# Loading and turning the first batch of q and k: 1 KB pieces, products into every fourth column, and a gate ahead of GpSimd's loads

## The chip, the cores and the metric

The kernel runs on one core of a Trainium2 chip. What counts is the device time of one execution in microseconds (us). The core's engines each work through a queue of their own: TensorE (PE) does matrix products, VectorE (DVE) and ScalarE (ACT) do elementwise work and empty PSUM, GpSimd (POOL) does some set-up and issues most loads, SyncE (SP) issues the other transfers. Sixteen DMA engines move the data.

## The reference

Attention over a sliding window with a distance bias, followed by a token mixer:

```python
B, H, S, D = 8, 8, 576, 64
scores = (q @ k^T) / 8                       # per batch and head
rel = i - j;  mask = (0 <= rel < 128)
scores = where(mask, scores - slope[h] * |rel|, -1e9)
x = softmax(scores) @ v                      # then (B, S, H*D) = (8, 576, 512)
W = ((x @ w_q) @ (x @ w_k)^T) / 8            # d_hyper 64
out = relu(W @ x) @ w_out                    # float32
```

q, k and v are float32, 256 bytes for each token of a head.

## The kernel before, in words

The 576 tokens of a batch are cut into four blocks of 128 and a tail of 64; the tails of two batches share tiles. The work of a batch is a set of small operations, each with a name of kind, batch and part:

- L: a load. Lq, Lk, Lv bring a block of q, k or v, Lt the tails of q and k. GpSimd issues them, with a change of type to fp16 on the way (`nat` for q and k, `vt` for v). Only batch 0's blocks of q and k are loaded by SyncE as fp32 into `natf` (`lf`, line 549) and cast to `nat` by VectorE or ScalarE (Cq, Ck, lines 365 and 367).
- TQ: 16 TensorE transposes per block turn `nat` so that head_dim lies on partitions (`add_tq`, line 361); ETQ empties PSUM into `qkT` (lines 371, 373). TT and ETT do so for the tails. From batch 1 on, one TQ takes two blocks.
- QK (g, u): scores of block g for half u of the heads; EXP on ScalarE (line 674, 128x1024); MUL by the bias tile on VectorE (line 681). `bias` is made on ScalarE from a mask that GpSimd builds, and `biasl` on VectorE from `bias`.
- PV: probabilities times v; X (lines 723, 724) normalises into `x`.
- XT, EXT turn `x`; WQ, EWQ, WK, EWK, G, EG are the mixer's small products; MX and RM give the relu (lines 835, 837); OUT times `w_out`, EO empties it into `osb` (lines 365, 367), DO writes it out (lines 913, 916).

The order on every engine is fixed when the kernel is built: a list scheduler (`Order.solve`) takes the operations with estimated costs, and where several could go next, the one with the lowest number in the table `WANT`. Each engine then runs its queue in that order and waits by semaphores. PSUM is four pairs of banks that the scheduler also assigns. `keep_busy` puts filler products (`fill`, 128x512) ahead of a TensorE operation for which the plan has a gap, in the first 30 us of the plan; the number comes from the gap divided by an assumed duration, 0.43 before `COLD` and 0.216 after it. The fillers write the bank of the operation that follows them, so they wait for that bank to be empty.

The outputs of batches in `LATE` are held in the pool `late` (18 slots, `HELD`, shared with the eight `natf` tiles) and written by GpSimd after all its loads (`d.deps += issues`); the others are written by SyncE. GpSimd's loads also wait for the eighth load before them to land. `pads` (GpSimd memsets of `xtl` and `xT`) must be done before its loads of q, k, v.

Of the kernel before, what the change touches and what calls it, by code (L numbers as in the profile page):

```python
# [14 lines left out]
P = 128  # L15
S = 576
D = 64
H = 8
# [19 lines left out]
HELD = 18  # L38
LATE = (2, 3, 4, 5)
COLD = 8.0  # L40
# [4 lines left out]
    "ident": -516.89, "idh": -64.27, "iota": -947.82, "dist": -823.27, "zeros": -897.48,  # L45
# [251 lines left out]
def kernel(  # L297
# [302 lines left out]
    def add_tq(b, ns, want):  # L600
# [21 lines left out]
        for n in ns:  # L622
            evt[b, n] = ev
# [380 lines left out]
```

## Time and profile before

| | |
|---|---|
| runs | 146.66 us median of 3 (146.28 to 148.61) |
| the profiled execution | 147.05 us, its span 145.3 us |
| busy: PE, DVE, ACT, POOL | 126.8, 116.7, 114.3, 104.8 us |
| DMA packets | 117447, of them 113072 under 512 bytes |
| loads of `natf`, 256 KB each | 8, issued by SP from 0.74 to 8.26 us, 3.0 to 8.0 us to landing |
| loads by GpSimd | first of `natt` at 5.73 us, last issue done at about 105.4 us |
| first EXP | 10.74 us |
| last product | ends about 141.5 us |

In the lines of the profile a time in us is followed by a duration, the engine, the line of the kernel (L674), the operation, the tile written and the tile read, and a count; in brackets stands how long the engine was idle before it, and what ended that. PEclk is the clock granted to TensorE in tenths. The windows give for a stretch the busy time of each engine with the number of instructions. The chain of waits is followed back from the last instruction.

### The profile page before, as it was taken

How to read it: one execution, taken by the hardware profiler on the slowest of the kernel's cores; microseconds unless marked ns; L12 is line 12 of the kernel's file. 1: busy time of each engine (PE TensorE's matmuls, PEld its weight loads, DVE VectorE, ACT ScalarE, POOL GpSimd, SP SyncE). 2: the span in 40 equal slices, each digit the busy share in tenths (PEclk: the TensorE clock that was granted, in tenths of full speed). 3: DMA queues.
4: the chain of work that ended last, by engine and by line, in shares of the span. 5: the costliest groups of instructions: out<-in, count | busy, mean ns of one | idle time of the engine just before them, and what ended most of it. 6: DMA issues, size and time to landing. Idle time of an engine off the chain costs nothing.

```text
span 145.3 us, 5428 instructions
## 1 busy us (share of the span) xinstructions
PE 126.8 (87%) x2315; PEld 80.0 (55%) x2315; DVE 116.7 (80%) x256; ACT 114.3 (79%) x169; POOL 104.8 (72%) x139
## 2 busy tenths in 40 slices
PE   6858858888997899779998997989999999999990
PEld 2224546645774458645674575647767657566340
DVE  6977997599839698959979999799999999991410
ACT  3727895599588976899599986999889989956751
POOL 5999678999986997578999999998977701230000
PEclk9986999999999999999999999999999999999999
DMA  4999999999999999999999999999999941155255
GB/s 103 262 182 180 159 154 144 149 173 154 190 251 186 157 183 218 247 179 155 156 155 156 157 154 157 154 154 151 146 213 399 363 171 72 77 144 207 83 162 202
DMA packets 117447, 25.64 MB, mean 177 GB/s; under 512 B 113072, under 2 KB 114096, under 8 KB 117424
## 3 DMA queue, kind: packets, MB, share of 16 engines
q0 software_dynamic: 106336, 18.49, 155.3%
q1 hardware_dynamic: 11088, 6.82, 16.6%
q8 instruction: 18, 0.29, 0.8%
q14 instruction: 5, 0.04, 0.1%
HBM read 29.62 MB, written 9.44 MB: 269 GB/s over the span
## 4 chain that ended last, share of the span: by engine, by line
PE 48%; DVE 16%; ACT 16%; POOL 7%; DMA 6%; issue 4%; POOLq 0%; DVEq 0%; ACTq 0%
PE pair L358 41%; ACT pt L674 10%; PE pair L361 7%; DMA vt<-in_v_dram 6%; DVE pt L681 3%; DVE x L724 3%; POOL nat L501 2%; DVE rm L837 2%; ACT qkT L371 2%; DVE xT L373 2%; DVE qkT L373 1%; POOL vt L516 1%; DVE inv L723 1%; POOL natt L508 1%; DVE xtl L724 1%
## 5 line engine op out<-in xcount | busy, mean ns | idle before, releaser
L674 ACT ACTIVATE pt<-pair 128x1024 f16<-128x1024 f32 x64 | 62.8, 1038 | 6.1 <-PE pair L358 5.8
L681 DVE TENSOR_TENSOR pt<-pt,bias 128x1024 f16<-128x1024 f16 x48 | 31.7, 683 | 3.3 <-ACT pt L674 3.1
L516 POOL DMA_DIRECT2D vt<-in_v_dram x32 | 29.7, 949 | 3.7 <-DMA nat<-in_k_dram 1.9
L358 PE MATMUL pair<-wout_sb,rm 128*128 128x512 f16 (+1 forms) x132 | 31.5, 373 | 0.7 <-ACT pt L674 0.5
L501 POOL DMA_DIRECT2D nat<-in_q_dram x28 | 25.9, 931 | 3.3 <-DMA vt<-in_v_dram 1.1
L501 POOL DMA_DIRECT2D nat<-in_k_dram x28 | 25.7, 925 | 1.6 <-DMA vt<-in_v_dram 0.5
L358 PE MATMUL pair<-qkT 64*128 64x256 f16 (+2 forms) x320 | 22.8, 254 | 4.0 <-ACT qkT L371 2.6
L358 PE MATMUL pair<-vt,pt 128*128 128x65 f16 x512 | 22.6, 193 | 1.4 <-DMA vt<-in_v_dram 1.0
L358 PEld LDWEIGHTS <-pt 128*128 128x128 f16 x576 | 20.0, 97 | 5.8 <-issue 2.5
L724 DVE TENSOR_TENSOR x<-pair,inv 128x512 f16<-128x512 f32 x32 | 22.1, 691 | 1.1
L365 ACT COPY osb<-pair 128x512 f32<-128x512 f32 (+1 forms) x25 | 14.8, 590 | 6.9 <-PE pair L358 6.7
L371 ACT COPY qkT<-pair 128x1024 f32<-128x1024 f32 (+2 forms) x19 | 16.0, 842 | 4.5 <-PE pair L361 3.5
L358 PEld LDWEIGHTS <-qkT 64*128 64x128 f16 x320 | 11.2, 95 | 12.4 <-issue 5.9
L358 PEld LDWEIGHTS <-rm 128*128 128x128 f16 x132 | 11.4, 97 | 12.0 <-issue 1.1
L913 POOL DMA_DIRECT2D out_dram<-osb x16 | 8.8, 558 | 11.0 <-DVE osb L367 5.4
L361 PEld LDWEIGHTS <-nat 64*128 64x128 f16 x512 | 9.4, 96 | 6.8 <-issue 4.6
L361 PE MATMUL pair<-identh,nat 64*128 64x64 f16 x512 | 11.2, 192 | 1.8 <-DVE x L724 0.4
L358 PE MATMUL pair<-fill 128*128 128x512 f16 x23 | 9.0, 531 | 3.1 <-DVE qkT L373 1.2
L358 PE MATMUL pair<-xT,wqq_sb 128*128 128x256 f16 (+1 forms) x64 | 10.3, 287 | 0.8 <-DVE xT L373 0.8
L681 DVE TENSOR_TENSOR pt<-pt,biasl 128x1024 f16<-128x1024 f16 x16 | 10.8, 683 | 0.2 <-ACT pt L674 0.2
L837 DVE TENSOR_SCALAR rm<-pair 128x512 f16<-128x512 f32 x16 | 10.5, 681 | 0.1
L367 DVE COPY osb<-pair 128x512 f32<-128x512 f32 (+1 forms) x12 | 8.0, 665 | 2.8 <-PE pair L358 2.7
(65 smaller groups left out, 162.7 us busy)
## 6 DMA issues: line engine op xcount, KB each, us to landing
vt<-in_v_dram POOLq DMA_DIRECT2D x32, 128.0 KB, 6.6
out_dram<-osb POOLq DMA_DIRECT2D x16, 256.0 KB, 4.6
out_dram<-osb SPq DMA_DIRECT2D x15, 256.0 KB, 5.4
nat<-in_k_dram POOLq DMA_DIRECT2D x28, 128.0 KB, 6.4
nat<-in_q_dram POOLq DMA_DIRECT2D x28, 128.0 KB, 6.4
natf<-in_q_dram SPq DMA_DIRECT2D x4, 256.0 KB, 4.5
natf<-in_k_dram SPq DMA_DIRECT2D x4, 256.0 KB, 4.8
out_dram<-osb SPq DMA_DIRECT2D x6, 128.0 KB, 2.4
```

Of the source, the lines that this page charges most:

```text
L358: hold(nc.tensor.matmul(*a, **k))
L361: hold(nc.tensor.transpose(*a))
L365: hold(nc.scalar.copy(out_ap, in_ap))
L367: hold(nc.vector.tensor_copy(out=out_ap, in_=in_ap))
L371: hold(nc.scalar.copy(out_ap.bitcast(FP32), in_ap.bitcast(FP32)))
L501: return lambda: nc.gpsimd.dma_start(out=nat_s[b % NNAT][j][n], in_=src[b, :, P * n:P * n + P, :].transpose([1, 0, 2]))
L516: return lambda: nc.gpsimd.dma_start(out=vt_s[b % NV][t][:, :, 0:D], in_=v[b, :, P * t:P * t + P, :].transpose([1, 0, 2]))
L674: nc.scalar.activation(out=pt[:, 0:1024], in_=two(s.bank).rearrange("p e c -> p (e c)"), func=AF.Exp, scale=SCALE)
L681: ENG2[o.eng].tensor_tensor(out=pt[:, 0:1024], in0=pt[:, 0:1024], in1=bt, op=ALU.mult)
L724: nc.vector.tensor_tensor(out=x[r].rearrange("p (g h d) -> p g h d", g=2, h=4), in0=pxv[r, :, :, 0:64], in1=inv[r].unsqueeze(3).broadcast_ ...
L837: hold(nc.vector.tensor_scalar(out=out_ap, in0=in_ap, scalar1=0.0, scalar2=WSCALE, op0=ALU.max, op1=ALU.mult))
L913: q.dma_start(out=out[b, P * st:P * st + P, c], in_=osb)
```

## The change

Batch 0's blocks of q and k come in by another layout. A 256 KB block of q or k is read so that a partition holds four consecutive tokens of a pair of heads: two transfers of 128 partitions (one for each head of the pair), each partition one piece of 1 KB. The cast puts the two heads of a token side by side. TQ then no longer transposes: for each of the four token positions a product of `nat` with the identity writes 64 columns to every fourth fp32 column of PSUM, so that the tokens come out in order, one PSUM bank for each half of the head pairs. Each bank is emptied by an instruction of its own (ETQ0.n.0 and ETQ0.n.1), and a QK of half u waits for its half alone.

SyncE's loads are issued in order of blocks, and a new GpSimd copy of one column of the third load's tile (`seen`) stands ahead of all of GpSimd's loads. Batch 1 joins the batches whose outputs GpSimd writes late; the pool has 23 slots, and every full-width output tile comes from it. `COLD` and a term of `keep_busy` change: 56 fillers instead of 23. The table `WANT` is new throughout, and with it the order on all engines. In the built order these matter for the start:

- GpSimd: `pads` first, then iota, identity and mask, then the copy into `seen`, then the loads; `wq_sb`, which was the first load, is the 15th; vt02, which was the tenth, is the 16th; all eight blocks of batch 1's q and k are within the first twelve.
- ScalarE: the load of the activation table stands behind a wait for the second transfer of the first block, then Cq0.0, then the bias.
- VectorE: Ck0.0, biasl1, ETQ0.0.0, Cq0.1, biasl0, Ck0.1, ETQ0.1.0, Cq0.2, Ck0.2.
- TensorE: 11 fillers, TQ0.0, 5 fillers, TQ0.1, 5 fillers, QK0.0 (two), 4 fillers, TQ0.2, 4 fillers, PV0.0, QK0.1.1, TT0, QK0.1.0, 9 fillers, TQ0.3, PV0.1.
- SyncE: from the fifth block on, each transfer waits until the transfer eight before it has landed.

```diff
-HELD = 18
-LATE = (2, 3, 4, 5)
-COLD = 8.0
+HELD = 23
+LATE = (1, 2, 3, 4, 5)
+COLD = 6.0
+GATE = (0, 1)
...
     def keep_busy(op, last):
         gap = op.start - max(last, op.bank_free, 0.6) - 0.15
-        n = int((gap + 0.3) / (0.43 if op.start < COLD else 0.216)) if gap > 0.1 else 0
+        n = int((gap + 0.5) / (0.43 if op.start < COLD else 0.216)) if gap > 0.1 else 0
...
     def load(name, want, emit, occ, serve, deps):
-        issue = add(*name, want, {"POOL": (occ, occ + 1.5)}, deps, lambda o: emit())
+        issue = add(*name, want, {"POOL": (occ, occ + 1.5)}, [*deps, *gate], lambda o: emit())
...
         def lf(j, n):
             natf = spool.tile([P, DM], FP32, name="natf", tag="late", bufs=HELD)
-            src = (q, k)[j][0, :, P * n:P * n + P, :].transpose([1, 0, 2])
+            src = (q, k)[j][0, :, P * n:P * n + P, :].rearrange("(c e) (g r) d -> e c g (r d)", e=2, r=4)

             def em(o):
-                nc.sync.dma_start(out=natf.rearrange("p (h d) -> p h d", h=H), in_=src)
+                for e in range(2):
+                    nc.sync.dma_start(out=natf[:, 256 * e:256 * e + 256], in_=src[e])

             def cv(o):
-                cp(o.eng, nat_s[0][j][n].rearrange("p h d -> p (h d)"), natf)
-
-            d = add("L" + "qk"[j], 0, f"f{n}", next(i), {"SP": (0.92, 1.55)}, [], em)
-            d = od.add("Q", 0, n, 0.0, {"Q": (0.92, 1.7)}, [d], lambda o: None)
+                cp(o.eng, nat_s[0][j][n].rearrange("p (r e) d -> p e r d", e=2),
+                   natf.rearrange("p (e r d) -> p e r d", e=2, r=4))
+
+            d = add("L" + "qk"[j], 0, f"f{n}", next(i), {"SP": (0.68, 1.3)}, first[-1:], em)
+            first.append(d)
+            d = od.add("Q", 0, n, 0.0, {"Q": (0.66, 1.2)}, [d], lambda o: None)
+            if (j, n) == GATE:
+                gate.append(add("gate", "", "", -50, {"POOL": (0.1, 0.12)}, [d],
+                                lambda o: nc.gpsimd.tensor_copy(out=seen, in_=natf[:, 0:1])))
...
+    def add_tq0(n, want):
+        def quad(o, h):
+            return one((o.bank[0], h)).rearrange("p (j c t) -> p j c t", j=2, c=2)
+
+        def em(o):
+            for j in range(2):
+                for i in range(4):
+                    for h in range(2):
+                        r = slice(64 * h, 64 * h + 64)
+                        mm(quad(o, h)[:, j].rearrange("p c (g i) -> p i c g", i=4)[:, i],
+                           nat_s[0][j][n][r, 2 * i:2 * i + 2, :].rearrange("p a b -> p (a b)"), identh[r, r],
+                           start=True, stop=True)
+
+        t = add("TQ", 0, n, want, pe(0.47), [loads[0, 0, n], loads[0, 1, n], idh], em, banks=2, mode=1)
+        tq[0, n] = t
+        evt[0, n] = []
+        for h in range(2):
+            def ev(o, h=h):
+                cp(o.eng, qkT_s[0][:, :, 2 * h:2 * h + 2, P * n:P * n + P], quad(t, h))
+
+            evt[0, n].append(add("ETQ", 0, f"{n}.{h}", want + 0.6, EV(0.60, 0.69), [t], ev, frees=[t], half=h))
...
-        need = [evt[b, g], evt[b, g + 1]] if g < 3 else [evt[b, 3], ett[b]]
+        need = [evt[b, g][u], evt[b, g + 1][u] if g < 3 else ett[b]]
...
-            held = b in LATE
-            box["o"] = spool.tile([P, n], FP32, name=f"osb{n}", tag="late" if held else f"osb{n}",
-                                  bufs=HELD if held else 5 if n == DM else 2)
+            box["o"] = spool.tile([P, n], FP32, name=f"osb{n}", tag="late" if n == DM else f"osb{n}",
+                                  bufs=HELD if n == DM else 2)
...
-        for ns in ([0], [1], [2], [3]) if b == 0 else ([0, 1], [2, 3]):
+        for n in range(4) if b == 0 else ():
+            add_tq0(n, base(b, 0) - 4 + 1.5 * n)
+        for ns in ([0, 1], [2, 3]) if b else ():
             add_tq(b, ns, base(b, 0) - 4 + 1.5 * ns[0])
```

More of the change, by code (lines that the diff above doesn't have):

```diff
@@ L37 @@
 LAG = 0.5
-HELD = 18
-LATE = (2, 3, 4, 5)
-COLD = 8.0
+HELD = 23
+LATE = (1, 2, 3, 4, 5)
+COLD = 6.0
+GATE = (0, 1)
 WANT = {
-    "ident": -516.89, "idh": -64.27, "iota": -947.82, "dist": -823.27, "zeros": -897.48,
[153 rows of a table removed]
+    "ident": -331.55, "idh": -57.5, "iota": -566.58, "dist": -425.66, "zeros": -434.25, "zerop":
[152 rows of a table added]
 }
@@ L313 @@
     ppool = ctx.enter_context(tc.tile_pool(name="psum", bufs=1, space=bass.MemoryType.PSUM))
+    seen = cpool.tile([P, 1], FP32, name="seen")
     fill = cpool.tile([P, 512], F16, name="fill")
@@ L530 @@
     wts = wto = None
-    late, issues = [], []
+    late, issues, gate, first = [], [], [], []
     loads = {}
@@ L622, in add_tq @@
         for n in ns:
-            evt[b, n] = ev
+            evt[b, n] = [ev, ev]
     def add_tt(pr, want):
```

305 rows, old and new, of the table WANT are left out of this document.

## The prediction

> **What bounds the kernel now.** I read the page, then the chain of waits, the timeline of the first 40 us, the busy time by windows and the DMA issues.
>
> ```profile
> PE 126.8 (87%) x2315; PEld 80.0 (55%) x2315; DVE 116.7 (80%) x256; ACT 114.3 (79%) x169; POOL 104.8 (72%) x139
> PEclk9986999999999999999999999999999999999999
> ...
> PE 48%; DVE 16%; ACT 16%; POOL 7%; DMA 6%; issue 4%; POOLq 0%; DVEq 0%; ACTq 0%
> ```
> ```profile
> 0.00:37.00 37.00, 28.84 (x439) 16.41 (x440) 30.20 (x87) 26.03 (x39) 32.28 (x49) 0.95 1.84 166
> 37.00:141.50 104.50, 97.94 (x1878) 63.63 (x1875) 86.48 (x170) 87.66 (x130) 72.56 (x91) 1.00 1.73 179
> ```
> The second fence (PE, PEld, DVE, ACT, POOL, clock, DMA share, GB/s) splits the run. From 37 us to the last product at 141.5, TensorE is idle 104.50 - 97.94 = 6.6 us: it sets the pace. In the first 37 us it is busy 28.8, 9.0 of it fillers (the page's group of 23), so some 19.8 us is work: about 17 us go in the start, where the change lies.
>
> ```profile
> 12.99 8.91 DMA vt<-in_v_dram
> ```
> ```profile
> 4.38 2.56 ACT L468 ACTIVATE bias<-wm 128x256 f16<-128x256 f32 x8 [2.36 <-POOL wm L426]
> 4.55 1.31 DVE L430 CAST identh<-ident 128x128 f16<-128x128 f32 x1
> 9.45 0.59 ACT L371 COPY qkT<-pair 128x512 f32<-128x512 f32 x1 [2.00 <-PE pair L361]
> 10.74 1.94 ACT L674 ACTIVATE pt<-pair 128x1024 f16<-128x1024 f32 x2 [0.71 <-PE pair L358]
> ...
> 21.94 0.64 PE L358 MATMUL pair<-vt,pt 128*128 128x65 f16 x16 [0.74 <-DMA vt<-in_v_dram]
> 23.86 1.96 ACT L674 ACTIVATE pt<-pair 128x1024 f16<-128x1024 f32 x2 [1.74 <-PE pair L358]
> 28.46 0.64 PE L361 MATMUL pair<-identh,nat 64*128 64x64 f16 x32
> 30.65 5.60 ACT L674 ACTIVATE pt<-pair 128x1024 f16<-128x1024 f32 x6
> ```
> Two limits follow each other. Up to the first EXP at 10.74, it is the row load, cast, turn, evacuation. Then it is GpSimd's load stream: the chain's DMA piece ends in PV0.2 at 21.94, and TQ1.2 at 28.46 has the stream's 17th load under it; six of batch 1's eight EXPs come only after it, and end at 36.25.
>
> **The change, part by part.** *Loads.* Each of eight 256 KB loads becomes two of 128 pieces of 1 KB.
>
> ```profile
> q1 hardware_dynamic: 8320, 2.10, 40.6%
> ```
> ```profile
> q1 hardware_dynamic: 11088, 6.82, 16.6%
> ```
> ```profile
> L913 SPq DMA_DIRECT2D out_dram<-osb x17: 332/332/530, 35.8 to 142.2; - x17
> ```
> The first row is of 0 to 25 us: 40.6% of 25 us is 10.15 us of 16 engines for eight loads in 256-byte pieces, 1.27 us each. Over the run (second row) 24.1 - 10.15 = 13.97 us go to 4.72 MB, or 18 pieces of 256 KB in 2 KB rows, 0.78 us each. 1 KB lies between: I take 0.85, 8 x 0.42 = 3.4 us of DMA time saved (bounds 0 and 3.9). Issues on SP: 16 x 0.33 and gaps, 5.8 us, against the last issue's end at 8.26 before. From the fifth load on, SP also waits for a semaphore lane, that is for loads 1 to 4 to land; with 1 MB under way that costs nothing while it feeds the engines. Landing: 3.0 us for the first load now, 2.0 at least for an output; I take 2.4, so both halves of the first are there at 3.5 (3.1 to 4.1), the last load at about 9.5 (8.5 to 12) against 15.2 now.
>
> *Gate.* The copy into `seen` waits for the third load's first half, about 4.7. GpSimd's own work ahead of it (pads 1.5, iota 0.36, ident 0.5, mask 0.8, no weight load of 0.68) ends about 4.2. Behind it queue all its loads, so its first leaves at 4.8 against 5.73. With SP's 3.4 us less in their way and that 0.9 us, the 17th load lands about 24.5 instead of 28, and the order changes: both rounds of batch 1's q and k are now within the first 12 (about 19 to 20), the wait before TQ1.2 goes; vt02 becomes the 16th (23 to 25), and PV0.2 now stands behind QK1.1. wq_sb, first of all before, comes 15th; its reader wqq has moved too. Each us that the third load is late is one for the whole stream.
>
> *ScalarE.* In the built order the table load, which ran at 0.73 under nothing, stands behind the wait for the first load's second half, ahead of Cq0.0. Its row says 1.28 us: 3.5 + 1.3 + 0.6 gives Cq0.0 done at 5.4, the bias (2.56) at 8.0 instead of 6.94, the first half evacuation at 8.6. TQ0.0 itself hides it: the eleven fillers ahead end at 6.06. By the Trainium skill (ScalarE: Activation LUTs, What ACT_TABLE_LOAD costs) a switch of table also drains for about 1.38 us; the row shows 1.28 and ScalarE then waits, so no run here shows the drain. By it the estimate would be some 1.4 us later here, and the sum 148.5.
>
> *Turning.* TQ0 keeps 16 products of 64 columns per block: 4 x 0.4 us. Writing every fourth fp32 column is in no row; between nothing and twice the time (1.6 us in all), I take nothing, since columns, not bytes, set the rows (0.19 us for fp32 and fp16 outputs alike). Evacuations double: four more of 128x512 fp32, two on ScalarE (0.60 each) and two on VectorE (0.69), 2.6 us, all in the walk below. The permuted cast I take at 0.5 (rows 0.41 to 1.46).
>
> *Pads moved first* end the 1.31 us cast of identh (a like cast takes 0.41 at least), which ran under those memsets: Ck0.0 can end at 4.95. *33 more fillers*, put by a warm pitch of 0.213 us, fall in gaps but stand before real work.
>
> *Walk.* VectorE: biasl1 waits for bias1 (6.7), to 7.45; ETQ0.0.0 8.15; Cq0.1 8.65; biasl0 9.2; Ck0.1 9.75. TensorE: five fillers after the evacuation at 8.6, TQ0.1 to 10.2, five fillers to 11.25 over the two halves of ETQ0.1 (10.95), QK0.0.1 to 11.7: first EXP 11.75, 1.0 later than now. TQ0.2 stands behind four fillers that need EXP0.0.1's bank (12.8), TQ0.3 behind nine and behind Ck0.3 (about 18.2): batch 0's EXPs end about 24.5 against 20.86. But no load is late then: eight EXPs, ETQ1.2 and EWQ0.0 are 9.6 us, so batch 1's end at 34.1 against 36.25. VectorE, from 19.4, has 16.6 us (X, EXT, MULs, ETQ1.0, EWK0) and 1.4 of waits: MUL1 done at 37.4 against 36.97. EWK0 lies at 35.4 in that row, so MX0 starts about 37.2 (29.0 now), OUT0 at 40.5 (33.55 now).
>
> TensorE's account at 40: before, beyond MX0, QK1 and PV1.0, it has done four OUT (4.1), PV1.1 to 1.3 (1.9), XT1.0 (0.4): 6.4 us. After, at 40.5: QK2.0 (0.6), TQ2.0 (0.64), four PV (2.5): 3.75. Backlog 2.65 + 0.5 = 3.1 us. What takes it back: of the 6.6 us that TensorE waits later, a backlog fills between 0 and 3.1; I take 1.6, as neither row is nearer. In the tail the built order has two OUT (2 x 1.04) before the last QK that stood behind it, and one PV (0.64) after it: 1.4 less on the last 20 us, of which I count 1.1.
>
> *Outputs of batch 1* go to GpSimd's end: six issues more, 26 x 0.54 = 14 us from 105.4, and 3.9 us of DMA time leave the stretch about 50 us, where TensorE waits for no load. Both are hidden: by the run to 141.5, and batch 6's evacuations, from 129.6, need slots of the first eight of them, landed about 115. Without that cover each would cost an issue, 0.54.
>
> **Sum**: +3.1 - 1.6 - 1.1 = +0.4 us, so the profiled execution of 147.05 (span 145.3, 1.75 around it) becomes 147.45; the median of the runs, 146.66, lies 0.39 lower: 147.1. Against 146.66 I call it no change; 2% is about what a measurement of this kernel can tell from none.
>
> **Rivals.** *The load stream was the whole limit.* For: 1.74 us of ScalarE's idleness ends in PV0.2's wait, and TQ1.2's lateness parts batch 1's EXPs by 4.8 us. Against: the first EXP is late for other reasons. If the first EXP starts by 10.7, so that the walk's 3.6 us of lateness stays below 1, the 3.4 us of DMA time and part of the 0.9 come through: 3.9 off, 142.8. *The start turns into a backlog that is never taken back*: fillers at the slow clock. For: PEclk falls to 0.5 from about 9.7 to 13.2 now, and a filler then takes 0.44 instead of 0.213 from start to start. The 14 fillers up to TQ0.2, and nine before TQ0.3, would add 23 x 0.23 = 5.3 us, of which I count 2.3, for the ten before the first EXP. It decides if that EXP starts beyond 13: 146.66 + 3.1 - 1.1 + 2.3 = 151.0. By the Trainium skill (TensorE: Matmul & The Clock Gate, Part 4: PE-mode transpose) transposes do not count as busy for the clock; products do, so by that page the clock would hold and this rival go. The trace agrees as far as the clock falls after a stretch of transposes, 6.2 to 9.4. *The gate holds nothing back*, because GpSimd reaches it after the load has landed (memsets slower beside VectorE's): the loads start as late as now, 0.9 later than summed, hidden by 12 loads landing about 20 for a need at 24: 147.1 again.
>
> **Chances.** Forecast 0.42, first rival 0.26, second 0.27, third 0.05. Within 2% (143.7 to 149.6) are the forecast and the third: 0.47. The forecast's own range is 145.0 to 149.2 (backlog taken back wholly and an early landing, or not at all and a late one). The range for 8 in 10 reaches to both others: 143.0 to 150.8.
>
> **What would show it.** Right: the table load at 3.1 to 4.1, first EXP 11.2 to 12.5, TQ1.2 with no wait for a load, batch 1's EXPs done at 33 to 35, MX0 near 37. Wrong: a first EXP before 10.7, MX0 before 33, TensorE's clock below 0.9 between 9 and 20, or TensorE's idle time after 37 us far from 5 us.

## The result, and the profile after

The changed kernel takes 162.55 us (median of four runs, 162.41 to 162.65) beside 146.77 for the kernel before in the same comparison: a ratio of 1.1087, interval 1.1056 to 1.1118. It is 11% slower. The prediction said no change, and its range ended at 150.8. (The profiled execution of the run s32, below, took 149.52 us beside a median of 148.70 for all its executions, so its start alone is read closely.)

The page of the changed kernel, the lines that answer to those shown of before (busy time by engine, the granted clock in 40 slices, the chain's shares):

```profile
PE 135.9 (85%) x2348; PEld 83.7 (52%) x2348; DVE 117.6 (73%) x258; ACT 114.9 (72%) x171; POOL 108.0 (67%) x146
...
PEclk9965599689999999999999999999999999999998
...
PE 55%; DMA 15%; DVE 12%; ACT 9%; issue 4%; SPq 1%; POOL 1%; DVEq 0%; ACTq 0%
```

TensorE is busy for 9.1 us more than before (135.9 against 126.8); that is not more work, since the page's group of fillers alone has grown from 9.0 to 19.5 us. The granted clock is low in more slices, and the DMA share of the chain has gone from 6% to 15%. The busy time by windows of the changed kernel (PE, PEld, DVE, ACT, POOL, granted clock, DMA share, GB/s) says in which part of the run this lies:

```profile
0.00:42.00 42.00, 27.13 (x283) 12.37 (x284) 19.40 (x66) 16.14 (x25) 20.84 (x35) 0.84 1.09 104
42.00:157.00 115.00, 108.82 (x2066) 71.30 (x2064) 98.20 (x193) 98.25 (x147) 87.15 (x112) 1.00 2.01 178
```

From 42 us on TensorE idles 115.00 - 108.82 = 6.2 us, as little as the 6.6 us of before from 37 on. So the loss is complete by 42 us: TensorE then has 108.82 - 97.94 = 10.9 us more left than the kernel before had at 37, five us earlier. The timeline of ScalarE in the changed kernel (start, duration, engine, line, operation, count, and in brackets the idle time before it and what ended it) shows it grow:

```profile
6.60 1.28 ACT L366 ACT_TABLE_LOAD   x1 [6.60 <-DMA natf<-in_q_dram]
7.89 0.62 ACT L366 CAST nat<-natf 128x512 f16<-128x512 f32 x1
8.42 2.55 ACT L469 ACTIVATE bias<-wm 128x256 f16<-128x256 f32 x8
...
19.55 1.94 ACT L703 ACTIVATE pt<-pair 128x1024 f16<-128x1024 f32 x2 [2.21 <-PE pair L359]
...
28.06 0.62 ACT L366 CAST nat<-natf 128x512 f16<-128x512 f32 x1 [2.81 <-DMA natf<-in_q_dram]
...
35.78 3.77 ACT L703 ACTIVATE pt<-pair 128x1024 f16<-128x1024 f32 x4 [0.76 <-PE pair L359]
```

The first block has landed at 6.60, where the prediction had 3.5; the first EXP starts at 19.55 and not at 11.75; batch 0's eight EXPs end at 39.55 and not at 24.5 (20.86 before). Two windows of one us before, the same two of the changed kernel, then its SyncE timeline and the row of SyncE's queue over 0 to 25 us (packets, MB, share of 16 engines) say why the blocks are late:

```profile
3.00:4.00 1.00, 1.00 (x4) 0.32 (x3) 0.81 (x15) 0.00 (x0) 0.46 (x2) 1.00 1.23 262
5.00:6.00 1.00, 1.00 (x3) 0.15 (x1) 1.00 (x2) 1.00 (x5) 1.00 (x4) 1.00 1.28 289
```
```profile
3.00:4.00 1.00, 1.00 (x4) 0.33 (x3) 0.82 (x11) 0.00 (x0) 0.59 (x3) 1.00 0.25 82
5.00:6.00 1.00, 0.96 (x3) 0.15 (x1) 0.00 (x0) 0.00 (x0) 0.00 (x0) 1.00 0.27 93
```
```profile
0.74 1.35 SPq L551 DMA_DIRECT2D natf<-in_q_dram  x2
...
5.10 2.80 SPq L551 DMA_DIRECT2D natf<-in_k_dram  x2
...
17.66 4.20 SPq L551 DMA_DIRECT2D natf<-in_k_dram  x2
```
```profile
q1 hardware_dynamic: 1704, 1.69, 22.6%
```

The share adds up the times of all packets, so it can pass one. Though several transfers have been issued and have not landed, it stays at 0.25 to 0.27 from 3 to 12 us, at 82 to 95 GB/s; before, the one-us windows from 3 to 7 have 1.17 to 1.28 at 236 to 289 GB/s. A share of 0.25 to 0.27 of sixteen is 4.0 to 4.3 packets under way at a time: it looks as if the transfers ran on four of the sixteen engines. SyncE's issues stretch from 1.35 us for two to 2.80 in the fourth block and 4.20 in the eighth, so the last leaves at 21.9.

### The profile page after: what moved, and what is told of

Its sections match the earlier page's. It is cut to its first block, busy times and chain, and to the rows that moved or that the text cites. A ratio compares the mean times of both kernels' runs of the same rounds, so it can differ in the third digit from the quotient of the medians.

```text
span 160.6 us, 5508 instructions
## 1 busy us (share of the span) xinstructions
PE 135.9 (85%) x2348; PEld 83.7 (52%) x2348; DVE 117.6 (73%) x258; ACT 114.9 (72%) x171; POOL 108.0 (67%) x146
## 2 busy tenths in 40 slices
DMA packets 110919, 25.64 MB, mean 160 GB/s; under 512 B 104816, under 2 KB 107888, under 8 KB 110896
## 4 chain that ended last, share of the span: by engine, by line
PE 55%; DMA 15%; DVE 12%; ACT 9%; issue 4%; SPq 1%; POOL 1%; DVEq 0%; ACTq 0%
PE pair L359 48%; DMA natt<-in_q_dram 10%; PE pair L362 7%; DMA natf<-in_q_dram 5%; ACT pt L703 4%; DVE pt L710 4%; DVE rm L866 3%; DVE x L753 2%; ACT rm L864 2%; SPq L551 1%; DVE inv L752 1%; ACT rmt L864 1%; ACT qkT L372 1%; POOL natt L509 1%; POOL vt L517 1%
## 5 line engine op out<-in xcount | busy, mean ns | idle before, releaser
L517 POOL DMA_DIRECT2D vt<-in_v_dram x32 | 28.8, 907 | 3.5 <-DMA nat<-in_q_dram 1.2
L359 PEld LDWEIGHTS <-pt 128*128 128x128 f16 x576 | 20.8, 97 | 7.1 <-issue 3.8
L359 PE MATMUL pair<-vt,pt 128*128 128x65 f16 x512 | 23.6, 194 | 0.5 <-ACT qkT L372 0.2
L359 PE MATMUL pair<-fill 128*128 128x512 f16 x56 | 19.5, 498 | 3.4 <-ACT pt L703 1.3
L359 PEld LDWEIGHTS <-rm 128*128 128x128 f16 x132 | 11.1, 97 | 11.9 <-issue 1.2
L941 POOL DMA_DIRECT2D out_dram<-osb x20 | 10.8, 545 | 4.4 <-ACT osb L366 2.5
L368 DVE CAST nat<-natf 128x512 f16<-128x512 f32 x6 | 2.9, 480 | 14.7 <-DMA natf<-in_k_dram 11.2
L359 PEld LDWEIGHTS <-fill 128*128 128x128 f16 x56 | 6.1, 119 | 12.2 <-issue 8.1
L372 ACT COPY qkT<-pair 128x1024 f32<-128x1024 f32 (+1 forms) x13 | 11.2, 870 | 0.9 <-PE pair L359 0.7
L366 ACT CAST qkT<-pair 128x512 f16<-128x512 f32 x4 | 2.3, 580 | 11.3 <-PE pair L359 11.3
L359 PE MATMUL pair<-identh,nat 64*128 64x64 f16 x64 | 3.6, 274 | 7.7 <-DVE nat L368 5.1
```

The costliest lines, as they stand in the source:

```text
L359: hold(nc.tensor.matmul(*a, **k))
L366: hold(nc.scalar.copy(out_ap, in_ap))
L372: hold(nc.scalar.copy(out_ap.bitcast(FP32), in_ap.bitcast(FP32)))
L517: return lambda: nc.gpsimd.dma_start(out=vt_s[b % NV][t][:, :, 0:D], in_=v[b, :, P * t:P * t + P, :].transpose([1, 0, 2]))
L941: q.dma_start(out=out[b, P * st:P * st + P, c], in_=osb)
```

## The experiments

Theory 1: the source of a transfer is now four head pairs, each of 32 groups of tokens, and a transfer is spread over as many DMA engines as its outermost dimension allows, here four. Theory 2: the products, their fp32 columns with a step of four, and the fillers make the start long. Theory 3: the gate ahead of GpSimd's loads does. By the Trainium skill (DMA: Bandwidth & Descriptors, Why a DMA increments its semaphore by 16 and not by 1), a transfer uses the largest number of engines, at most 16, that divides the slowest dimension longer than one on both of its sides. The trace agrees, with a share of 0.25 to 0.27 for 4 outermost here and 0.46 to 0.55 for 8 and 0.65 to 0.79 for 32 in the first two runs below.

**Outermost dimension 32 (s32) and 8 (s8).** Line 547 alone; the pieces stay at 1 KB, 128 to a transfer. Batch 0's tokens then come out in another order, so of these two, and of s32free, rows2k, early and fills, only the time is read.

```diff
-  ....rearrange("(c e) (g r) d -> e c g (r d)", e=2, r=4)
+  ....rearrange("(c e) (g r) d -> e g c (r d)", e=2, r=4)   # s32
+  ....rearrange("h (e g r) d -> e h g (r d)", e=2, r=4)     # s8
```

> The changed kernel with one edit: the two outer dimensions of the source of each of batch 0's transfers stand the other way round, 32 groups of tokens outside and 4 head pairs inside (the tile's partitions go in that order too; batch 0's tokens then come out in another order, the rest of the work is the same). Still two transfers a block, pieces of 1 KB, the same waits. Theory 1, that a transfer is spread over as many DMA engines as divide the outermost dimension of both its sides (4 in the changed kernel, 16 here): the DMA share before GpSimd's loads rises from 0.25-0.27 to over 0.8 and the rate from 89 to 250-330 GB/s, the first cast starts at 3.5 to 5 us after a table load instead of 7.9, the eighth cast at 9 to 12 instead of 32.8, first EXP 10.5 to 12.5 instead of 19.55, and the time falls from 162.6 to 145-149. Theory 2, that strided 1 KB pieces are slow in themselves: share and rate as in the changed kernel, time 162. Theory 3, that the gate costs the time: 162 as well, since the gate is untouched.

> The changed kernel with the source cut so that the outermost dimension of each transfer is 8 (heads), then 16 groups of 4 tokens: two transfers a block, 64 tokens of all heads each, pieces of 1 KB (batch 0's tokens come out in another order). Theory 1: 8 of 16 engines, DMA share 0.5 and about 180 GB/s before GpSimd's loads, a block every 1.5 to 1.9 us, the eighth cast at 14 to 17 us, first EXP 12 to 14.5, time 148-153, between the two others. Theories 2 and 3: 162.

Measured: s32 148.70 us, ratio to before 1.0058 (1.0006 to 1.0109); s8 151.68 us, ratio 1.0326 (1.0273 to 1.0378). The windows 3 to 4 and 5 to 6 us of s8, then of s32:

```profile
3.00:4.00 1.00, 1.00 (x4) 0.33 (x3) 0.82 (x11) 0.00 (x0) 0.59 (x3) 1.00 0.53 176
5.00:6.00 1.00, 0.32 (x2) 0.00 (x0) 0.00 (x0) 1.00 (x1) 0.00 (x0) 1.00 0.48 147
```
```profile
3.00:4.00 1.00, 1.00 (x4) 0.33 (x3) 0.82 (x11) 0.00 (x0) 0.59 (x3) 1.00 0.79 214
5.00:6.00 1.00, 0.05 (x1) 0.00 (x0) 0.38 (x1) 0.99 (x2) 0.00 (x0) 1.00 0.70 209
```

The share is a quarter, a half, and 0.65 to 0.79. The packets themselves are no slower in the changed kernel: over its first 11 us, 733 packets take 20.6% of sixteen engines, 0.206 x 16 x 11 / 733 = 49 ns each, and in s32 from 3 to 6 us 648 take 71.5%, or 53 ns each. So it is not the place of the pieces in memory that makes them slow; fewer are under way at a time. One swapped pair of letters takes the ratio from 1.1087 to 1.0058, that is 0.1029 of the 0.1087 lost, or 95% (by s32's interval, 90 to 99%). Theory 1 is shown, and theory 2 has at most what is left; theory 3 is taken up next. In s8 TensorE also runs at a granted clock of 0.50 from 8 to 14 us, so its time holds more than the loads' lateness. In s32 it is SyncE's issues that limit, as its timeline shows: each pair takes 1.25 us from start to end, and the eighth pair ends at 11.1.

```profile
2.10 1.25 SPq L551 DMA_DIRECT2D natf<-in_k_dram  x2
...
4.31 1.28 ACT L366 ACT_TABLE_LOAD   x1 [4.31 <-DMA natf<-in_q_dram]
...
12.55 1.94 ACT L703 ACTIVATE pt<-pair 128x1024 f16<-128x1024 f32 x2 [0.93 <-PE pair L359]
...
21.49 3.77 ACT L703 ACTIVATE pt<-pair 128x1024 f16<-128x1024 f32 x4 [0.76 <-PE pair L359]
```

**No gate (nogate, on the changed kernel; s32free, on s32).** GpSimd's copy reads the identity tile.

```diff
-  nc.gpsimd.tensor_copy(out=seen, in_=natf[:, 0:1])
+  nc.gpsimd.tensor_copy(out=seen, in_=ident32[:, 0:1])
```

> The changed kernel, but the copy ahead of GpSimd's loads reads the identity, which is there, instead of the third load's tile: nothing holds the loads back, the order is the same. Theory 1: GpSimd's first load leaves at 4.4 instead of 11.1 us, but batch 0's blocks still come through 4 engines, every 3.1 to 4.2 us or slower since GpSimd's packets are in the way; the eighth cast stays at 32 us or later, the time at 158-164. Theory 3: the loads come 6.7 us sooner, and with them the time falls to 152-156.

> s32 with the gate's copy reading the identity tile instead of the third load, so GpSimd's loads start as soon as its own set-up is done. Theory 1 (on four engines the gate was worth 3.6 us because GpSimd's packets stood in the way; on sixteen engines SP's issues at 0.62 each are the limit and leave room): first GpSimd load at 4.4 to 5.0 instead of 6.24, batch 0's EXPs as in s32 within 0.5 us, later loads 1.3 us earlier, time within 0.5 us of s32 or up to 1 us shorter. Rival (the gate protects batch 0's blocks whatever the number of engines): the casts and the first EXP are 0.7 to 2 us later than 12.55 and the time 0.7 to 2 us over s32.

Measured: nogate 166.19 us, ratio 1.1269 (1.1198 to 1.1340); s32free 150.05 us, ratio 1.0183 (1.0107 to 1.0260). GpSimd's and ScalarE's timelines of nogate, ScalarE's of s32free, and TensorE's of s32 and then of s32free:

```profile
4.27 0.18 POOL L562 COPY seen<-ident 128x1 f32<-128x1 f32 x1
...
23.19 1.94 ACT L703 ACTIVATE pt<-pair 128x1024 f16<-128x1024 f32 x2 [2.10 <-PE pair L359]
```
```profile
14.95 1.94 ACT L703 ACTIVATE pt<-pair 128x1024 f16<-128x1024 f32 x2 [2.03 <-PE pair L359]
```
```profile
9.20 1.24 PE L359 MATMUL pair<-fill 128*128 128x512 f16 x5 [2.30 <-ACT qkT L366]
10.38 0.62 PE L359 MATMUL pair<-identh,nat 64*128 64x64 f16 x16
```
```profile
9.03 2.29 PE L359 MATMUL pair<-fill 128*128 128x512 f16 x5 [2.04 <-ACT qkT L366]
11.26 1.04 PE L359 MATMUL pair<-identh,nat 64*128 64x64 f16 x16
```

The copy comes at 4.27 in place of 10.97, GpSimd's loads start 6.7 us earlier, and the run is longer: the ratio is 0.0182 higher, about 2.7 us. Theory 3 falls: the gate helps. With GpSimd's loads in their way, the blocks come later: the cast of the fourth starts at 19.37 in place of 15.63, that of the eighth at 36.94 in place of 32.79, and the first EXP is 3.6 us later.

With sixteen engines the time of s32free is longer too, against what theory 1 expected of it: the ratio is 0.0125 higher, about 1.8 us, with intervals that just meet. But its trace shows another cause than its rival named. The casts of the first four blocks start within 0.4 us of those in s32 (the fourth at 9.98, there 10.07). What comes later is TensorE's work: its granted clock is 0.50 from 8 to 14 us, where s32 has 1.00, and five fillers take 2.29 us in place of 1.24, the 16 products 1.04 in place of 0.62. The first EXP starts 2.4 us later by that. Whether the missing gate brought on the slow clock is not shown, nor is what the gate is worth with sixteen engines.

**Four transfers per block (four32).** Each head pair goes out by itself, with 32 groups outermost.

```diff
-  ....rearrange("(c e) (g r) d -> e c g (r d)", e=2, r=4)
+  ....rearrange("(c e) (g r) d -> c g e (r d)", e=2, r=4)
-  for e in range(2):
-      nc.sync.dma_start(out=natf[:, 256 * e:256 * e + 256], in_=src[e])
+  for c in range(4):
+      nc.sync.dma_start(out=natf[32 * c:32 * c + 32].rearrange("p (e x) -> p e x", e=2), in_=src[c])
```

> The changed kernel with four transfers a block instead of two, one for each group of two heads: 32 partitions by two pieces of 1 KB, the outermost dimension 32 on both sides; layout, results and order as in the changed kernel. Theory 1: 16 engines each, share over 0.7; 32 issues of 0.33 us and more make SyncE the limit, the last leaves at 12 to 14 us, the eighth cast at 14 to 17, first EXP 11 to 13, time 146-151. Theories 2 and 3: 162 or more.

Measured: 151.74 us, ratio 1.0312 (1.0256 to 1.0367). SyncE's timeline of four32:

```profile
2.59 1.84 SPq L551 DMA_DIRECT2D natf<-in_k_dram  x4
```

An issue of 64 KB takes 0.46 us, one of 128 KB 0.62: halving the size does not halve the issue. 32 issues last to 17.2, the DMA share is only 0.48 to 0.56, and the first EXP starts at 13.72. Theory 1 had put an issue at 0.33 us and the share over 0.7, and its 146 to 151 us was missed: 64 KB every 0.47 us is 139 GB/s, and the windows from 3 to 8 us show 128 to 148.

**One transfer of 2 KB pieces (rows2k).** Eight tokens of a head make a piece, 16 groups are outermost.

```diff
-  ....rearrange("(c e) (g r) d -> e g c (r d)", e=2, r=4)   # two transfers
+  ....rearrange("h (g r) d -> g h (r d)", r=8)              # nc.sync.dma_start(out=natf, in_=src)
```

> A block in one transfer of 128 pieces of 2 KB, outermost dimension 16 on the source's side, in place of two of 128 pieces of 1 KB; partitions then hold (group of eight tokens, head) and batch 0's products turn tokens and heads in a mixed order, so only the time is read. Theory 1 (in s32 SP's issues, 0.62 each and 1.25 per block, are what limits the loads): eight issues of 0.35 to 0.7 instead of sixteen, the last by 7 instead of 11.1, DMA share 0.75 to 1.0 in 3 to 7 us, the gate's copy at 4.8 to 5.5 instead of 6.12, the eighth cast 1 to 3 us earlier unless the planned order holds it, time 0 to 1.5 us under s32's 148.7. Rival (the engines' own rate for this pattern limits, issues only wait for them): last landing within 0.7 us of s32's and share as there, 0.65 to 0.79, time as s32 within 0.4 us.

Measured: 146.50 us, ratio 0.9972 (0.9924 to 1.0021). SyncE's and ScalarE's timelines, and a window, of rows2k:

```profile
2.10 0.60 SPq L550 DMA_DIRECT2D natf<-in_q_dram  x1
```
```profile
0.74 1.28 ACT L366 ACT_TABLE_LOAD   x1 [0.74 <-PEq L1017]
```
```profile
3.00:4.00 1.00, 1.00 (x4) 0.33 (x3) 0.82 (x11) 0.00 (x0) 0.59 (x3) 1.00 1.06 311
```

The issue of 256 KB takes 0.60, as that of 128 KB took 0.62; all are out by 5.9, and the share reaches 1.06 at 311 GB/s: theory 1 of this run holds for the loads. But the gate's copy comes at 6.73, later than in s32 (6.12); that more blocks now share the engines is the likely reason. The casts come earlier (the fourth at 8.41, in s32 at 10.07), yet the first EXP is at 12.92 and batch 0's EXPs end at 25.64, later than in s32: TensorE's granted clock is 0.50 from 8 to 11 us here. So the start does not show why the run is shorter than s32, and the two intervals overlap. One thing it does show: with one transfer per block, the table load is back at 0.74, as in the kernel before; in the runs with two or four transfers per block it stands behind a wait, at 4.13 to 6.60. The parts of a block are what pushed the table load there.

**The table load early (early).** s32, with a small Exp first on ScalarE.

```diff
+  nc.scalar.activation(out=early, in_=fill[:, 0:1], func=AF.Exp)
```

> s32 (16 engines, ratio to before 1.006) with ScalarE's table load taken from behind the first block's wait: one Exp of a 128x1 column of the zeroed filler tile is put first on ScalarE. Theory 1 (the table load's 1.28 us lies on the path of the start, and nothing drains behind it): the load of the table stands near 1.2, Cq0.0 starts at 4.3 instead of 5.61, the bias ends near 7.4 instead of 8.6, the first EXP moves from 12.55 to 11.3 to 12.1 (fillers planned ahead of it stay), and the run is 0.2 to 1.0 us faster than s32: 147.7 to 148.5. Rival (Ck0.0, which waits for its own load until 5.62, and the planned order set the first EXP): the bias ends earlier, the first EXP stays within 0.3 of 12.55, time as s32 within 0.3 us.

Measured: 146.78 us, ratio 0.9974 (0.9932 to 1.0015). ScalarE's timeline of early:

```profile
0.74 1.28 ACT L485 ACT_TABLE_LOAD   x1 [0.74 <-PEq L1020]
...
4.52 0.62 ACT L367 CAST nat<-natf 128x512 f16<-128x512 f32 x1 [2.28 <-DMA natf<-in_q_dram]
...
11.46 1.94 ACT L705 ACTIVATE pt<-pair 128x1024 f16<-128x1024 f32 x2 [0.92 <-PE pair L360]
```

Cq0.0 starts 1.09 us earlier and so does the first EXP, as theory 1 said; the ratio is 0.0084 lower, 1.2 us, where it had 0.2 to 1.0. This pair alone does not show that the time came from the table load, since the intervals overlap and s32's executions differ by clock: of the seven that enter its ratio, five with a mean granted clock of 0.984 to 0.988 took 148.41 to 148.89 us, and two at 0.996 took 147.01 and 146.77, like the ten of early (0.986 to 1.00). The pair perm and permearly, below, does. By the Trainium skill (ScalarE: Activation LUTs, What ACT_TABLE_LOAD costs), a switch to another set of tables takes a load of about 1.28 us and a drain of about 1.38. The trace agrees on the load, 1.28, and shows no drain behind it: in the changed kernel Cq0.0 starts at 7.89, 0.01 us after the table load that began at 6.60 and took 1.28.

**Fewer fillers (fills).** s32 with `COLD = 8.0` and `gap + 0.3`, as before.

> s32 with the number of fillers worked out as in the kernel before (COLD 8.0, gap + 0.3), so some 30 products fewer in the first 30 us. Theory 1 (with 16 engines the clock stays at 1.00 and the fillers ahead of real work cost their own time in the queue): first EXP some 0.4 to 0.8 earlier than 12.55, batch 0's EXPs end 0.5 to 2 us earlier than 25.26, time 0 to 1.0 us under s32's 148.7. Rival (the fillers are what holds the clock): granted clock of 0.5 to 0.8 in some stretch between 8 and 20 us, as in the kernel before between 9.7 and 13.2, first EXP not earlier, time equal or 0.5 to 2 us longer.

Measured: 147.55 us, ratio 1.0005 (0.9958 to 1.0052). The clock falls to 0.50 from 10 to 12 us and the first EXP comes 0.63 later, at 13.18, as the rival said; but batch 0's EXPs end at 25.25 against 25.26, and the run is not longer. What the fillers cost and what the clock costs without them cannot be told apart at this resolution.

**Sixteen engines, with the tokens in order (perm, permearly, permfew).** A product takes all 128 rows, and the identity's columns with a step of four put them in order; permearly adds the early table load, permfew also the fillers' number of before.

```diff
-  nat_s[0][j][n][r, 2 * i:2 * i + 2, :]..., identh[r, r],
+  nat_s[0][j][n][:, 2 * i:2 * i + 2, :]..., identh.rearrange("p (g c) -> p c g", c=4)[:, 2 * h:2 * h + 2, :],
```

> s32's loads (outermost 32, 16 engines) with batch 0's tokens and heads in their right places again: each product takes all 128 rows of nat and, as its moving operand, 64 columns of the identity with a step of 4. Theory 1 (the products go by columns, not by rows or by the step of the operand): 16 products per block in 0.6 to 0.7 warm as in s32, first EXP 12.3 to 12.9, time as s32 within 0.7 us: 148.0 to 149.4. Rival (an operand read with a step, or twice the rows, costs more): 16 products in 0.9 us or more warm, first EXP 0.5 to 1 later than 12.55, time 0.5 to 2 us over s32.

> perm with ScalarE's table load taken early as in the run early (a 128x1 Exp of the filler tile first). Theory 1 (the engines per transfer and the table load are the two things that the change lost; all else nearly cancels): first EXP 11.2 to 11.9, time 146.0 to 147.4, ratio to before 0.993 to 1.003, so no gain that can be told from none. Rival (the shorter start in early was worth more than its first run showed, as MX0 and OUT0 come earlier too): ratio 0.985 to 0.993.

> permearly with the number of fillers worked out as in the kernel before. Theory 1 (fillers and clock cancel, as in the run fills, where the first EXP came 0.6 later by the slow clock and batch 0's EXPs still ended at the same 25.2): granted clock 0.5 for 2 to 4 us between 8 and 13, first EXP 11.6 to 12.6, ratio within 0.005 of permearly's. Rival (the fillers stand ahead of real work at more than the clock is worth): batch 0's EXPs end 0.4 us or more earlier than permearly's, ratio 0.005 to 0.012 lower.

Measured: perm 148.88 us, ratio 1.0096 (1.0057 to 1.0134); permearly 147.37 us, ratio 1.0003 (0.9970 to 1.0037); permfew 146.47 us, ratio 0.9952 (0.9912 to 0.9992). TensorE's timeline of s32, then of perm:

```profile
14.58 0.62 PE L359 MATMUL pair<-identh,nat 64*128 64x64 f16 x16
```
```profile
14.95 1.12 PE L359 MATMUL pair<-identh,nat 128*128 128x64 f16 x16
```

perm's rival holds for the products: 0.5 us more per block. Batch 0's EXPs end at 26.33 in place of 25.26, but in the time it hardly shows: the ratio is 0.0038 higher, with overlapping intervals. Rows and step were changed together, so which of them it is stays open. permearly is no change against the kernel before, as theory 1 said. Against perm its ratio is 0.0093 lower, 1.4 us, the intervals lie apart, and both profiles have a granted clock of 1.00 through the start: here the early table load is shown to be worth its time. permfew differs from it by 0.0051 with overlapping intervals, and batch 0's EXPs end at 24.76 and 24.75 in the two, so no cause is claimed for that difference; the clock stayed at 1.00, against what was expected. permfew, with batch 0's tokens and heads in their places, lies half a per cent under the kernel before, with an interval that just excludes one; against the 2% that the prediction set for a change, that is none.

## Why the prediction was wrong, point by point

- **The step that failed: "8 x 0.42 = 3.4 us of DMA time saved", and with it the landings.** The engine time itself was sized well: 22.6% of 25 us is 5.65 us of 16 engines for 1.69 MB, 0.88 us per 256 KB against the 0.85 taken. But a share of 16 engines was read as elapsed time. On four engines 0.88 us is 3.5 us, eight blocks are 28 us, and the eighth cast waits until 32.8, where the sum had the last load landed at 9.5. The new access pattern was costed by the size of its pieces alone; its outermost dimension was not looked at, no rival had it, and the bounds (0 to 3.9 us saved) allowed no loss.
- **Landing of the first block, 3.1 to 4.1.** 6.60 with four engines, 4.31 with sixteen: even without the failed step this was 0.8 too early for the 3.5 taken. Some 0.65 of it is the issue of the second half, which ended at 2.06 in s32 and not at 0.74 + 2 x 0.33 = 1.40; the output rows were the wrong neighbours for it.
- **Issues of 0.33 us.** The rows of outputs (256 KB, 0.33) did not carry over: a load of 128 pieces took 0.62 us for 128 KB and 0.60 for 256 KB. Sixteen were to be out by 5.8; in s32 they last to 11.1.
- **The wait for a semaphore lane "costs nothing".** On the condition that came with it, that the engines are fed, it holds: the four engines had work throughout. It was the stretched issues that fed them; how much of the stretching is the lane's wait is open, since it begins in the third and fourth block, ahead of the first such wait.
- **The gate.** "Each us that the third load is late is one for the whole stream" was right in kind: the copy came at 10.97 and not at 4.7. But that it protects the blocks, and is worth about 2.7 us here, was not in the working.
- **The table load behind the wait.** Right in place and size, 1.28 us, with nothing behind it; taken away, it gives 1.4 us between perm and permearly.
- **The walk.** Where sixteen engines carry the loads (s32) it comes 0.3 to 1.6 us late but keeps its order: first EXP 12.55 (11.75), batch 0's EXPs end at 25.26 (24.5), no load late at TQ1.2, batch 1's EXPs end at 35.7 (34.1), MX0 37.5 (37.2), OUT0 41.7 (40.5). Two of its signs were missed even so, the first EXP by 0.05 us (11.2 to 12.5) and the end of batch 1's EXPs by 0.7 (33 to 35). The products' price, taken at nothing between 0 and 1.6, is some 0.2 us per block: 16 of them take 0.62, 16 transposes of before 0.41.
- **The account of the backlog.** early starts TensorE's mixer products at 36.9 where before has 29.0, ends batch 0's EXPs at 24.64 in place of 20.86, and takes as long as before. From 37 to 141.5 us TensorE is busy for 99.60 us in early and 97.94 before, and idle for 4.9 and 6.6: 1.7 us of work came later, and it all went into waits. The sum had 3.1 us of backlog, 1.6 of it filled into such waits and 1.1 won in the tail. The waits were sized right; the backlog came to 1.7, in a start that is 1.1 us shorter than that of s32; the tail's 1.1 is not shown. For s32 the forecast of +0.3% stands beside +0.6% measured, and how much of that nearness is luck stays open.
- **The slow clock.** The sign named for it came, 0.50 to 0.55 from 10 to 20 us in the changed kernel, while TensorE waited for blocks. By the Trainium skill (TensorE: Matmul & The Clock Gate, Part 4: PE-mode transpose) the prediction expected that products would hold the clock. The starts of s32 and early agree (1.00 up to 25 us). But s32 and fills had the same products up to 8 us, and only fills fell to 0.78 in the next two; s32free differs from s32 in GpSimd's copy alone, and fell to 0.50 from 8 to 14; and s32's own profile has 0.50 from 69 to 72 us. So products alone do not decide it, and the rival "fillers at the slow clock" was a real one: it is what made s32free's start 2.4 us later, and s32free's first EXP at 14.95 and its 150.05 us lie near what that rival gave (beyond 13, 151.0).

## What to carry to other kernels

Before a transfer's access pattern is changed, look at the outermost dimension on both of its sides, and keep it a multiple of 16 (16 in rows2k and 32 in s32 did); a larger piece does not pay for a quarter of the engines. In a profile, a DMA share that stays flat at 0.25 or 0.5 while transfers are queued is the sign. When an experiment's first products come later, look at the granted clock before the load is blamed. Every step that takes its duration from a share of 16 engines needs the question of how many of the sixteen do the work.

## What was not expected of the hardware

- The issue of a load on SyncE does not go by its bytes: 0.46 us for 64 KB in 64 pieces, 0.62 for 128 KB and 0.60 for 256 KB in 128 pieces. The number of pieces does not set it alone either: the first load of the kernel before, 256 KB in 1024 pieces, took 0.43.
- Transfers on few engines hold up GpSimd's loads as well: the tail load `natt`, issued by GpSimd at 12.97 in the changed kernel, let TensorE wait 3.36 us until 29.54 for it, more than 16 us after its issue; over the whole run the median from issue to landing of such a load is 6.9 us, and in s32 the first two took 5.3 and 6.7.
- Sixteen products with 128 rows and an operand with a step of four took 1.12 us at the full clock, the same columns with 64 rows 0.62.
